# A direct column-tiled projection for the first head groups, split weight loads, and a gate logit carried as a column of v

## The chip, the cores and the metric

The kernel runs on one core of one Trainium2 chip. The time is the device time of one execution in microseconds (us). Executions of one kernel agree within one to two per cent, so a kernel is run several times and the median is given. A run more than 1.5% above the fastest of the same kernel is labelled slow, and slow runs are left out of ratios.

The engines are TensorE (PE; its weight loads are PEld), VectorE (DVE), ScalarE (ACT), GpSimd (POOL) and SyncE (SP, which here issues nearly all DMAs; its queue is SPq). Each works through a list of instructions of its own, in the order that the program gives. PEclk is the granted clock of TensorE; 1.0 is full speed. A DMA lands when its data has arrived; times to landing are counted from its issue.

## The reference, cut to what matters

The output mixes two branches of the same x (2048 rows of 640) by a gate: infini-attention (32 heads of 20, four segments of 512 rows, softmax inside a segment plus a memory of earlier ones) and a spectral filter (2-D FFT, a product, inverse FFT).

```python
x = A_x
g = sigmoid((x * gate_w).sum(-1, keepdims=True))     # one number per row
a = attention(x, wq, wk, wv, wo, beta)
b = irfft2(rfft2(x) * (w_r + 1j * w_i))
out = g * a + (1 - g) * b
# inside attention, for each of 4 segments of 512 rows and each of 32 heads:
q, k, v = x @ wq, x @ wk, x @ wv                     # 640 columns = 32 heads x 20
p = softmax(q @ k.T * scale + causal_mask)
o = sig(beta) * (phi(q) @ M) / (phi(q) @ z) + (1 - sig(beta)) * (p @ v)
M, z = M + phi(k).T @ v, z + phi(k).sum()
```

## The kernel before

The kernel is written as a list of operations with a priority each. A list scheduler turns it, before anything runs, into one fixed order per engine, by modelled costs and these priorities. So every edit can move instructions on every engine.

```python
    TSTART, TEND, F_START, F_END = 13.8, 215.6, 27.9, 227.1      # priorities: when the
    LEAD, LEAD_END, QK_LEAD, PV_LAG = 35.3, 2.6, 15.6, -2.0      # 80 exponentials are meant
    O_STEP, FIN = 1.5, (3.0, 1.0)                                # to run, and the rest round them
    def either(self, fn, n, r, w, prio, name="", after=()):      # FFT folds: DVE or GpSimd,
        return self.Sc.op({"dve": (fn, 75 + 0.6 * n, 90.0),      # whichever the cost model
                           "pool": (fn, 100 + 1.95 * n, 90.0)}, ...)    # finds earlier free
```

The start loads x transposed and then the weights, all on the SP queue; the whole of wq has to land before the first projection.

```python
    def loads(self):
        self.xt_load(0, 0.0)                     # xT of segment 0, a DMA transpose
        ...
        wload(self.wq, self.wq_d, "wq", 0.1)     # 128 x 5 x 640
        wload(self.wk, self.wk_d, "wk", 0.2)
```

The heads are 20 rows high, and this kernel gives each of them 32 partitions of its own for the attention matmuls. So q and k go out to DRAM and come back in padded rows (qp, kp), four heads to a head group, four groups to a tile. Two groups are a pair, and one pair takes five exponentials of 128 x 2048. QK is the matmul in front of an exponential (q with k), PV the one behind it (the exponentials with v). A fold is an addition or subtraction of two halves of x before the forward transform.

```python
    def project(self, s):
        for half in range(2):
            tiles = (0, 1, 2) if half == 0 else (3, 4)
            for which in ("q", "k"):
                for t in tiles:
                    self.proj_tile(s, which, t, ...)   # 5 matmuls, eviction, store to q_scr/k_scr
                for j in range(4):                      # padded reload of four groups
                    self.dma(pad.ap(0, [L, 4], [1, L], p0=32 * j, np_=32), <scr rows>, ...)
        for i in range(4):
            self.v_tile(s, i, pv, xT, xb)
        self.gate(s, t_end, xT, xb)
```

The gate is 80 matmuls of one column for each segment, arranged so that the result already has the layout that the output needs (row 16p + 4a + q).

```python
    def gate(self, s, t_end, xT, xb):
        for a in range(4):
            for c in range(5):
                for q in range(4):                     # 32 rows each, stride 16
                    matmul(ps[32 * q, a], xT.ap(c * L + 4 * a + q, [16, 32]), gw.ap(c, [1, 1]), ...)
        z[0:4] = exp(-ps)                              # ACT, then three tiny DVE operations
```

The softmax here doesn't subtract the row's maximum and nothing guards it: scores larger than these inputs give would overflow.

Of the kernel before, what the change touches and what calls it, by code (L numbers as in the profile page):

```python
# [9 lines left out]
ACT = mybir.ActivationFunctionType  # L10
ALU = mybir.AluOpType
BF = dt.bfloat16
F32 = dt.float32

P = 128
S = 2048
D = 640
H = 32
DH = 20
NSEG = 4  # L20
L = 512
# [475 lines left out]
class Kern:  # L497
# [62 lines left out]
    def either(self, fn, n, r, w, prio, name="", after=()):  # L560

        return self.Sc.op({"dve": (fn, 75 + 0.6 * n, 90.0), "pool": (fn, 100 + 1.95 * n, 90.0)}, r=r, w=w, prio=prio, name=name, after=after)

# [11 lines left out]

    TSTART, TEND, F_START, F_END = 13.8, 215.6, 27.9, 227.1
    LEAD, LEAD_END, QK_LEAD, PV_LAG = 35.3, 2.6, 15.6, -2.0
    PH, MEM0, MEMU, O_BASE = 4.0, 5.5, 1.2, 13.2
    O_STEP, FIN = 1.5, (3.0, 1.0)

# [21 lines left out]
    def alloc(self):  # L602
# [5 lines left out]
        self.kd = nc.dram_tensor("k_scr", (NSEG, 656, L), BF)  # L608
        self.od = nc.dram_tensor("o_scr", (S, D), BF)

        self.Cp = T("Cp", [P, 3 * 4096])
# [27 lines left out]
        self.wo = T("wo", [P, 5 * D])  # L639
        self.wv = T("wv", [P, 5 * D])  # L640
        self.gw = T("gw", [P, 8])
        self.xT = [T(f"xT{i}", [P, 5 * L]) for i in range(2)]
# [20 lines left out]
        self.ebx = T("ebx", [P, 4 * H], F32)  # L663
        self.gz = T("gz", [P, 64], F32)
        self.rs = [T(f"rs{i}", [P, 16], F32) for i in range(4)]
        self.dn = [T(f"dn{i}", [P, 32], F32) for i in range(4)]
# [51 lines left out]
    def loads(self):  # L718
        x = self.x

        def wload(t, d, key, prio, pitch=D):
            self.dma(lambda: t.ap(0, [pitch, 5], [1, D]), lambda: dap(d, 0, [D, P], [P * D, 5], [1, D]),
                     P * 5 * D * 2, [], [self.b(key)], prio, name="ld_" + key)
        self.xt_load(0, 0.0)
        for nm, scr in (("q", self.qd), ("k", self.kd)):
            self.dma(lambda scr=scr: dap(scr.ap(), D * L, [656 * L, NSEG], [L, 16], [1, L]),
                     lambda: dap(self.tab["fcat"].ap(), 0, [16 * L, NSEG], [L, 16], [1, L]), 64 * L * 2, [], [self.b(nm + "tail")], 0.22,
                     name="ld_tail")
        wload(self.wq, self.wq_d, "wq", 0.1)
        wload(self.wk, self.wk_d, "wk", 0.2)  # L730
        self.dma(lambda: self.fcat.ap(0, [1, 512]), lambda: dap(self.tab["fcat"].ap(), 0, [512, P], [1, 512]),
                 P * 1024, [], [self.b("fcat")], 0.9, name="ld_fcat")
        for q in range(8):
            self.dma(lambda q=q: self.xsb.ap(q * 2 * D, [D, 2], [1, D]),
                     lambda q=q: dap(x, q * 2 * D, [16 * D, P], [D, 2], [1, D]),
                     P * 2 * D * 2, [], [self.b("xsb", q)], 1.0 + 0.2 * q, name="ld_x")
        self.dma(lambda: self.beta.ap(0, [1, H]), lambda: dap(self.beta_d, 0, [0, P], [1, H]), P * 64, [],
                 [self.b("beta")], 0.25, name="ld_beta")
        wload(self.wv, self.wv_d, "wv", 0.3, D)
        self.dma(lambda: self.gw.ap(0, [1, 5]), lambda: dap(self.gw_d, 0, [1, P], [P, 5]),  # L740
                 P * 5 * 64, [], [self.b("gw")], 2.8, name="ld_gw")
        self.dma(lambda: self.big.ap(0, [1, 3216]), lambda: dap(self.tab["big"].ap(), 0, [3216, P], [1, 3216]),
                 P * 6432, [], [self.b("big")], 5.0, name="ld_big")
        self.dma(lambda: self.hm.ap(0, [1, 880]), lambda: dap(self.tab["hmask"].ap(), 0, [880, P], [1, 880]),
                 P * 1760, [], [self.b("hm")], 6.0, name="ld_hm")
        wload(self.wo, self.wo_d, "wo", 60.0)
# [50 lines left out]
    def project(self, s):  # L797
        b = self.b
        xT = self.xT[s % 2]
        xb = b("xT", s % 2)  # L800
        t_end = self.texp(s, 0)
        lead = self.LEAD if s else self.TSTART
        t0 = t_end - lead
        span = lead - self.LEAD_END if s else 2.0
        if s > 0:
            self.xt_load(s, self.texp(s - 1, 0) + 6.0 if s > 1 else 10.0)
        k = 0
        for half in range(2):
            tiles = (0, 1, 2) if half == 0 else (3, 4)
            for which in ("q", "k"):  # L810
                for t in tiles:
                    self.proj_tile(s, which, t, t0 + span * k / 10.0, xT, xb)
                    k += 1
                pad = (self.qp if which == "q" else self.kp)[(2 * s + half) % self.NPAD]
                scr = self.qd if which == "q" else self.kd
                rb = [b(which + "d", s, t) for t in (tiles if half == 0 else (2, 3, 4))] + [b(which + "tail")]
                for j in range(4):
                    def dst(j=j, pad=pad):
                        return pad.ap(0, [1, 4 * L], p0=32 * j, np_=32) if False else pad.ap(0, [L, 4], [1, L], p0=32 * j, np_=32)

                    def src(j=j, scr=scr, half=half):
                        return dap(scr.ap(), s * 656 * L + (320 * half + 20 * j) * L, [L, 32], [80 * L, 4], [1, L])
                    self.dma(dst, src, 32 * 4 * L * 2, rb, [b(which + "p", (2 * s + half) % self.NPAD, j)],
                             t0 + span * k / 10.0, name="pad_" + which)
        for i in range(4):
            pv = t0 + span * (0.3 + 0.6 * i / 4)
            if s == 0:
                pv = 2.2 + 0.2 * i
            self.v_tile(s, i, pv, xT, xb)
        self.gate(s, t_end, xT, xb)  # L830

    def gate(self, s, t_end, xT, xb):

        b, z = self.b, self.gz
        bank = Bank(1, "gen")
        prio = t_end - 2.0
        items = []
        for a in range(4):
            for c in range(5):
                for q in range(4):  # L840
                    def th(a=a, c=c, q=q):
                        return (self.ps(bank, a, [1, 1], p0=32 * q, np_=32), xT.ap(c * L + 4 * a + q, [16, 32]), self.gw.ap(c, [1, 1]),
                                c == 0, c == 4, {"tile_position": (0, 32 * q)})
                    items.append((th, 1))
        self.mms(items, [xb, b("gw"), bank], [], prio, name="gate")
        self.one("act", lambda e: e.activation(z.ap(4 * s, [1, 4]), self.ps(bank, 0, [1, 4]), ACT.Exp, scale=-1.0), 4,
                 [bank], [b("ge", s)], prio, name="gate_exp")
        self.one("dve", lambda e: e.tensor_scalar(z.ap(16 + 4 * s, [1, 4]), z.ap(4 * s, [1, 4]), 1.0, None, ALU.add), 4,
# [6 lines left out]
    def proj_tile(self, s, which, t, prio, xT, xb):  # L855
# [10 lines left out]
        for c in range(5):  # L866
            self.mms([(lambda c=c: (self.ps(bank, 0, [1, L]), w.ap(c * D + t * P, [1, P]), xT.ap(c * L, [1, L]),
                                    c == 0, c == 4, {}), L)], [b("w" + which), xb, bank], [], prio, name="proj")
        self.Sc.op(self.copy_alts(lambda: qu.ap(0, [1, L]), lambda: self.ps(bank, 0, [1, L]), L),
# [28 lines left out]

    def v_tile(self, s, i, prio, xT, xb):
        b = self.b  # L900
        va, vb = self.va[s % 2], b("va", s % 2, i)
        for (h0, nh, w) in ((0, 25, 500), (25, 7, 140)):
            self.v_part(s, i, h0, nh, w, prio, xT, xb, va, vb)

    def v_part(self, s, i, h0, nh, w, prio, xT, xb, va, vb):
        b = self.b
        bank = Bank(1, "gen")
        for c in range(5):
            self.mms([(lambda c=c: (self.ps(bank, 0, [1, w]), xT.ap(c * L + i * P, [1, P]), self.wv.ap(c * D + h0 * DH, [1, w]),
                                    c == 0, c == 4, {}), w)], [b("wv"), xb, bank], [], prio, name="vproj")  # L910
        self.one("dve", lambda e: e.tensor_tensor(  # L911
            va.ap(i * H * VW + h0 * VW, [VW, nh], [1, DH]), self.ps(bank, 0, [DH, nh], [1, DH]),
            self.ebx.ap(H + h0, [1, nh], [0, DH]), ALU.mult), nh * DH, [bank, b("omgh")], [vb], prio, name="ev_v")
    def mem_read(self, s):
        b = self.b
# [54 lines left out]
    def qk_unit(self, s, pr, u, parts):  # L970
# [5 lines left out]
        for gp, js in parts:  # L976
            g = 2 * pr + gp
            pidx, gl = (2 * s + g // 4) % self.NPAD, g % 4
            qp, kp = self.qp[pidx], self.kp[pidx]
            rb += [b("qp", pidx, j) for j in range(4)] + [b("kp", pidx, j) for j in range(4)]  # L980
            for j in js:
# [290 lines left out]
```

## Time and profile before

| | before |
|---|---|
| time, median of 3 runs | 297.97 us (297.27 to 299.27) |
| span of the profiled run | 295.0 us |
| first exponential starts | 29.4 us |
| last exponential starts | 263.0 us |

From the page of the kernel before: busy us with the share of the span, then (parts in tenths, 40 slices of 7.4 us) PE and its granted clock.

```profile
PE 255.5 (87%) x3564; PEld 152.5 (52%) x3588; DVE 213.0 (72%) x510; ACT 199.8 (68%) x183; POOL 184.1 (62%) x259
...
PE   6797367799999688899999799999899999999690
...
PEclk9799755579999699999999799999999999999997
```

PE is the busiest engine. It has a thin stretch at the start, where its clock also drops, and is nearly full from then on. The table by stretch of the same kernel (busy us of PE, PEld, DVE, ACT, POOL with counts, then PEclk, DMA share, GB/s) puts numbers on that.

```profile
0.00:30.00 30.00, 24.14 (x109) 10.45 (x110) 11.43 (x24) 9.05 (x15) 13.14 (x16) 0.94 0.81 227
...
30.00:62.00 32.00, 21.05 (x315) 14.07 (x316) 29.85 (x58) 20.24 (x18) 22.83 (x31) 0.54 0.65 161
...
120.00:270.00 150.00, 143.77 (x2139) 86.22 (x2152) 117.61 (x291) 121.63 (x104) 104.30 (x150) 0.99 0.47 109
```

From 30 to 62 us DVE is busy 29.85 of 32 us and PE runs at about half clock; from 120 to 270 us PE is busy 96%. The chain of waits of the kernel before (start us, us, what) opens with the loads.

```profile
0.80 2.75 SPq L568
...
3.62 5.20 DMA wq<-in_A_wq_dram
...
8.86 9.26 PE psum L541 x35
...
274.52 4.42 DMA oTl<-on_115
...
282.93 5.23 DMA out_dram<-ot_83
```

The issue of the transpose comes first, then wq, which lands at 8.8 us; only then do real projections start. At the end, DMAs are what is waited for: a transpose of the attention's output (oTl) and a store of the final output. The timeline of the kernel before shows the first attention matmuls, the first exponential and one gate burst.

```profile
28.94 0.40 PE L541 MATMUL psum<-qp_107,kp_109 20*128 20x512 bf16 x4 [0.48 <-DMA kp_109<-k_scr]
...
29.38 1.88 ACT L1001 ACTIVATE ex<-psum 128x2048 bf16<-128x2048 f32 x1 [6.94 <-PE psum L541]
...
51.36 1.43 PE L541 MATMUL psum<-gw,xT_96 128*32 128x1 bf16 x80
```

The first pair waits for the padded reload of k, and a gate burst takes PE 1.43 us (the three others 1.41). The trace of the kernel before lacks 24 of its 3588 matmul records (x3564 against x3588 weight loads), all of them projections of 512 columns; this matters below, where busy times are compared.

### The profile page before, as it was taken

The page shows a single profiled execution, that of the slowest core. Times are in us where ns is not written, and L with a number is a line of the kernel's source. Part 1 is how long each engine was busy: PE and PEld are TensorE (multiplying, and loading weights), DVE is VectorE, ACT ScalarE, POOL GpSimd, SP SyncE. Part 2 cuts the span into 40 slices and gives each one's busy share as a digit, 9 for nine tenths or more (in the row PEclk, how much of TensorE's full clock was granted, in tenths as well). Part 3 has the DMA queues.
Part 4 walks back from the last instruction along what each step waited for, and adds up shares of the span by engine and source line. Part 5 has one row for each costly group of instructions (what it writes and reads, how often), then busy time and mean ns, then how long its engine had stood idle before and what let it go on. Part 6 is the DMA issues. An engine that isn't in the chain of part 4 may idle for free.

```text
span 295.0 us, 8701 instructions
## 1 busy us (share of the span) xinstructions
PE 255.5 (87%) x3564; PEld 152.5 (52%) x3588; DVE 213.0 (72%) x510; ACT 199.8 (68%) x183; POOL 184.1 (62%) x259
## 2 busy tenths in 40 slices
PE   6797367799999688899999799999899999999690
PEld 2343235574557446465656456555466555555370
DVE  0049999977987589698999898884769676765251
ACT  1170556668988377998889678879778987673220
POOL 6046478876968559699878869995655462633000
PEclk9799755579999699999999799999999999999997
DMA  7869991264975958755465954234633004375622
GB/s 170 289 173 267 270 256 35 55 149 129 224 171 129 219 95 200 172 127 144 114 140 160 162 151 117 74 108 71 176 111 118 17 2 49 89 109 118 124 83 65
DMA packets 60552, 40.07 MB, mean 136 GB/s; under 512 B 33464, under 2 KB 57304, under 8 KB 60504
## 3 DMA queue, kind: packets, MB, share of 16 engines
q1 hardware_dynamic: 60512, 39.51, 55.5%
q8 instruction: 28, 0.46, 0.7%
q14 instruction: 12, 0.10, 0.1%
HBM read 22.45 MB, written 9.96 MB: 110 GB/s over the span
## 4 chain that ended last, share of the span: by engine, by line
PE 49%; DVE 21%; DMA 8%; SPq 8%; ACT 5%; POOL 3%; issue 3%; DVEq 0%
PE psum L541 49%; ACT ex L1001 5%; SPq L568 5%; DVE xsb L792 4%; SPq L570 3%; DMA kp_109<-k_scr 2%; DVE Ac L551 2%; DVE Pt_66 L1143 2%; DMA out_dram<-ot_83 2%; DMA wq<-in_A_wq_dram 2%; DVE Pt_67 L1143 2%; DMA oTl<-on_115 1%; DVE va_111 L911 1%; POOL ex L1004 1%; DVE xf_118 L787 1%
## 5 line engine op out<-in xcount | busy, mean ns | idle before, releaser
L1001 ACT ACTIVATE ex<-psum 128x2048 bf16<-128x2048 f32 x80 | 150.0, 1875 | 40.1 <-PE psum L541 39.8
L1004 POOL TENSOR_SCALAR_AFFINE_SELECT ex<-ex 128x512 bf16<-128x512 bf16 x128 | 80.8, 649 | 44.3 <-ACT ex L1001 44.2
L541 PEld LDWEIGHTS psum<-va_111,ex 128*128 128x128 bf16 x640 | 23.6, 99 | 8.9 <-POOL ex L1004 1.5
L541 PE MATMUL psum<-va_111,ex 128*128 128x21 bf16 x640 | 25.8, 175 | 1.4 <-POOL ex L1004 1.1
L541 PE MATMUL psum<-qp_107,kp_109 20*128 20x128 bf16 (+3 forms) x256 | 18.3, 344 | 10.0 <-ACT ex L1001 5.4
L541 PEld LDWEIGHTS psum<-va_112,ex 128*128 128x128 bf16 x640 | 22.7, 96 | 6.8 <-issue 2.6
L541 PE MATMUL psum<-va_112,ex 128*128 128x21 bf16 x640 | 25.1, 173 | 0.6 <-DVE Pt_66 L1143 0.5
L541 PE MATMUL psum<-big,Ac 128*128 128x321 bf16 (+2 forms) x96 | 24.2, 343 | 0.3 <-DVE Pt_67 L1143 0.2
L541 PE MATMUL psum<-wv,xT_97 128*128 128x500 bf16 (+1 forms) x80 | 22.6, 302 | 0.5 <-DVE rs_129 L1029 0.2
L541 PE MATMUL psum<-big,Cp 128*128 128x321 bf16 (+1 forms) x96 | 20.2, 302 | 0.0
L541 PE MATMUL psum<-wv,xT_96 128*128 128x140 bf16 (+1 forms) x80 | 18.3, 301 | 1.1 <-DVE va_111 L911 0.8
L541 PE MATMUL psum<-fcat,xsb 128*128 128x128 bf16 x80 | 10.7, 302 | 7.9 <-DVE xsb L792 6.1
L541 PE MATMUL psum<-xT_96,wq 128*128 128x512 bf16 x45 | 15.3, 411 | 2.5 <-DMA wq<-in_A_wq_dram 2.5
L551 DVE CAST Cp<-psum 128x512 bf16<-128x512 f32 (+1 forms) x24 | 13.4, 575 | 5.0 <-PE psum L541 4.8
L541 PE MATMUL psum<-qp_108,kp_110 20*128 20x128 bf16 (+3 forms) x256 | 15.9, 301 | 0.4 <-ACT ex L1001 0.2
L541 PE MATMUL psum<-xT_97,wk 128*128 128x512 bf16 x43 | 15.5, 379 | 0.0
L1143 DVE TENSOR_TENSOR Pt_66<-psum,Wt_62 128x321 bf16<-128x321 f32 x32 | 14.4, 481 | 1.3 <-PE psum L541 1.0
L1036 POOL TENSOR_TENSOR on_115<-on_115,mem 128x320 bf16<-128x320 bf16 x16 | 12.8, 801 | 3.8 <-DVE on_115 L1031 3.6
L1143 DVE TENSOR_TENSOR Pt_67<-psum,Wt_63 128x321 bf16<-128x321 f32 x32 | 13.8, 485 | 1.5 <-PE psum L541 1.5
L891 POOL TENSOR_TENSOR phk_104<-phk_104,et_101 128x512 bf16<-128x512 bf16 x6 | 7.0, 1159 | 12.6 <-DVE et_101 L889 12.1
L541 PE MATMUL psum<-xT_96,wk 128*128 128x512 bf16 x46 | 14.7, 382 | 0.0
L551 DVE CAST G<-psum 128x321 bf16<-128x321 f32 x25 | 11.7, 487 | 4.1 <-PE psum L541 3.9
(193 smaller groups left out, 568.1 us busy)
## 6 DMA issues: line engine op xcount, KB each, us to landing
xsb<-in_A_x_dram SPq DMA_DIRECT2D x8, 320.0 KB, 5.0
qp_107<-q_scr SPq DMA_DIRECT2D x16, 128.0 KB, 3.1
kp_109<-k_scr SPq DMA_DIRECT2D x16, 128.0 KB, 2.8
qp_108<-q_scr SPq DMA_DIRECT2D x16, 128.0 KB, 3.7
kp_110<-k_scr SPq DMA_DIRECT2D x16, 128.0 KB, 3.0
tt_59<-tab_tt SPq DMA_DIRECT2D x6, 256.0 KB, 3.2
tt_60<-tab_tt SPq DMA_DIRECT2D x5, 256.0 KB, 3.9
tt_61<-tab_tt SPq DMA_DIRECT2D x5, 256.0 KB, 3.3
```

The lines of the kernel that those rows point to most:

```text
L541: h = e.matmul(o_, l_, r_, start=st, stop=sp_, **kw)
L551: alts["dve"] = (lambda e: e.tensor_copy(dst(), src()), 75 + 1.04 * n, 85.0)
L568: return e.dma_start_transpose(d_, s_)
L570: return e.dma_start(d_, s_)
L787: self.either(lambda e, r=r, op=op: e.tensor_tensor(xf.ap(r * 642, [321, 2], [1, 320]), xs.ap(o, [D, 2], [1, 320]), xs.ap(o + 320, [D, 2], ...
L792: self.either(lambda e, dst=dst, src=src, d0=d0, n=n, op=op: e.tensor_tensor(xs.ap(o + dst, [D, 2], [1, n]), xf.ap(src + d0, [321, 2], [1, ...
L891: fadd = lambda e: e.tensor_tensor(dst(), dst(), et.ap(0, [1, L]), ALU.add)
L911: self.one("dve", lambda e: e.tensor_tensor(va.ap(i * H * VW + h0 * VW, [VW, nh], [1, DH]), self.ps(bank, 0, [DH, nh], [1, DH]), self.ebx. ...
L1001: self.one("act", lambda e: e.activation(dst(), src(), ACT.Exp, scale=SC), 4 * width, [bank], [self.exb(s, g, j) for g, j in outs], prio - ...
L1004: self.one("pool", lambda e, g=g, j=j: e.affine_select(self.ex.ap(self.exo(s, g) + JOFF[j], [1280, 4], [1, P]), self.ex.ap(self.exo(s, g) ...
L1036: self.one("pool", lambda e, g=g: e.tensor_tensor(on.ap(80 * g, [D, 4], [1, 80]), on.ap(80 * g, [D, 4], [1, 80]), self.mem.ap(80 * g, [D, ...
L1143: self.one("dve", lambda e, r=r, ri=ri, Pt=Pt, Wt=Wt, bank=bank: e.tensor_tensor(Pt.ap((2 * r + ri) * 322, [1, KD]), self.ps(bank, 0, [1, ...
```

## The change

The intent is to take three things off the front and off PE. First, head groups 0 and 1 of segment 0 are projected straight into the padded layout by four column tiles of 32, without the trip through DRAM. Second, the first 192 columns of wq and wk come as separate loads on the ACT queue. Third, the gate's 80 matmuls go: gate_w becomes column 641 of the v weights, so the logit falls out of the v projection, and a small store and reload through DRAM turns it into the layout that the output needs. The constants of the schedule were tuned anew as well, and the cost that the scheduler assumes for a fold on DVE was raised. The diff, cut to its core:

```diff
-        return self.Sc.op({"dve": (fn, 75 + 0.6 * n, 90.0), "pool": (fn, 100 + 1.95 * n, 90.0)}, ...)
+        return self.Sc.op({"dve": (fn, 75 + 0.8 * n, 90.0), "pool": (fn, 100 + 1.95 * n, 90.0)}, ...)
-    TSTART, TEND, F_START, F_END = 13.8, 215.6, 27.9, 227.1
-    LEAD, LEAD_END, QK_LEAD, PV_LAG = 35.3, 2.6, 15.6, -2.0
-    PH, MEM0, MEMU, O_BASE = 4.0, 5.5, 1.2, 13.2
-    O_STEP, FIN = 1.5, (3.0, 1.0)
+    TSTART, TEND, F_START, F_END = 9.7, 206.1, 27.9, 227.1
+    LEADS, LEAD_END, QK_LEAD, PV_LAG = (35.3, 35.3, 35.3), 2.6, 15.6, -3.5
+    PH, MEM0, MEMU, O_BASE = 4.0, 5.5, 1.1, 13.2
+    O_STEP, FIN, V0, XT1 = 1.5, (0.8, 2.6), 2.9, 11.2
 ... loads
+        wload(self.wq, self.wq_d, "wqa", 0.0, D, 0, n0, "act")           # n0 = 192
+        wload(self.wk, self.wk_d, "wka", 0.01, D, 0, n0, "act")
+        wload(self.wq, self.wq_d, "wqb", 0.1, D, n0, D - n0)
+        wload(self.wk, self.wk_d, "wkb", 0.11, D, n0, D - n0)
 ... project, segment 0 only
+            for n_, (g, which) in enumerate(((0, "q"), (0, "k"), (1, "q"), (1, "k"))):
+                self.proj_direct(which, g, -0.5 + 0.1 * n_, xT, xb)
+    def proj_direct(self, which, g, prio, xT, xb):
+        for c in range(5):
+            for hh in range(4):                      # four column tiles, one after the other
+                matmul(ps(p0=32 * hh, np_=32), w.ap(c * D + (4 * g + hh) * DH, [1, 32]),
+                       xT.ap(c * L, [1, L]), tile_position=(0, 32 * hh))
+        copy(pad.ap(g * L, [1, L]), ps)
 ... gate
-        <80 one-column matmuls and one exp per segment>
+        self.dma(lambda: dap(self.gd.ap(), s * L, [1, P], [P, 4]), lambda: self.gr.ap(4 * s, [1, 4]), 512 * 64,
+                 [b("gr", s, i) for i in range(4)], [b("gd", s)], prio, name="st_g")
+        self.dma(lambda: z.ap(4 * s, [1, 4]), lambda: dap(self.gd.ap(), s * L, [1, 4], [16, 32], [4, 4]), 512 * 64,
+                 [b("gd", s)], [b("ge", s)], prio, name="ld_g")
 ... v_part
-        for (h0, nh, w) in ((0, 25, 500), (25, 7, 140)):
+        for (h0, nh, w) in ((0, 25, 500), (25, 7, 141)):
+        if h0:
+            activation(self.gr.ap(4 * s + i, [1, 1]), self.ps(bank, 140, [1, 1]), ACT.Exp, scale=-1.0)
```

## The prediction

> **What bounds it now.** The busy table has PE 255.5 us of 295, DVE 213, ACT 200 (150 of it the 80 exponentials, 1.88 us each), and the chain of waits is 49% PE. In windows there are two regimes. From 120 to 270 us PE is 96% busy at full clock: only less PE work shortens that. Before 120 us PE is idle 23 us and runs at half clock from about 33 to 62 us (granted clock 0.5).
>
> The start is a chain of latencies. The timeline has: transpose of x issued 0.8 us, wq issued behind it at 3.6 and landed at 8.8 (first real matmul 8.86); projections; store to DRAM; padded reload; first QK at 28.9; first exponential at 29.4. ACT is busy only 0.6 us with exponentials before 30 us. From 29 to 62 us DVE is the limiter (about 95% busy from 25 to 55: FFT folds, evictions), and exponentials come one per about 3.3 us there.
>
> **Removed.** (1) The DRAM round trip for head groups 0 and 1: their five exponentials can begin at about 11-13 us rather than 29.4. (2) The gate matmuls: 4 bursts of 80, 1.4 us each by the trace: 5.7 us of PE, some 4.3 of it where PE counts. (3) Waiting for the whole of wq: half-width pieces on a second issuing queue should land near the transpose of x, at 5.5-6.5 us. The Trainium skill (DMA: Bandwidth & Descriptors, "Issuing engines are not separate DMA queues") says a second queue saves only issue time, here about 3 us.
>
> **Added.** 80 column-tiled matmuls of 512 columns. In this trace four column tiles of 320 columns go by every 0.14-0.15 us (8 in 0.46 with the drain), so I estimate 0.22-0.24 us per four at full clock: 20 x 0.23 = 4.6 us, up to 9 if cold. Four evictions (0.6 us each), 12 more tiny exponentials on ACT for the gate (0.17 us each, 2 us), 8 small 4-byte gate DMAs, 1,280 more weight packets. The full projections still run, some 4 us later unless the earlier weights pay for it. Folds move from DVE to GpSimd (1.4 against 0.41 us alone).
>
> **On the critical path.** The exponentials start 17 us earlier, but most of that does not survive: PE is already 99% busy from 10 to 25 us, and the second pair of head groups still needs the round trip (ready near 29-31 us). What survives is one pair's attention work done in formerly idle PE and ACT time. That is about 8 us of full-clock PE (QK 2-3, PV 160 x 35 ns), taken from the later saturated stretch, plus 4 us of gate, less 3-4 us of pushed-back start work. About 9 us.
>
> **Prediction: 289 us, 8 in 10 between 282 and 295.** Faster by over 2%: 0.70; within 2%: 0.25; slower: 0.05.
>
> **Signs.** First exponential at 10-14 us; first five done by 26 us; the sixth at 30-34 us. Direct-projection matmuls start 55 ns apart. No gate bursts. PE still at half clock for part of 33-60 us because folds on DVE remain the limiter. Span from the last exponential to the end as before (about 30 us). PE idle before 120 us down by 8 us or more.
>
> **What would make it wrong.** The second pair's padded rows come 5 us or more later; then the gain halves. A queue stall of SP behind the gate's store and reload. Odd-element rows of the V weights slowing the 500-column matmuls. Or, upward: PE stays warm through 33-60 us, worth several us more.

## The result, and the profile after

| | before | after |
|---|---|---|
| time, median of 4 runs | 298.62 us (297.27 to 299.64) | 334.29 us (329.44 to 334.79) |
| ratio of the fast runs | 1 | 1.112 (95%: 1.095 to 1.128) |
| first exponential starts | 29.4 us | 17.3 us |
| last exponential starts | 263.0 us | 301.5 us |

Ratios here are the mean time of one kernel's fast runs over that of the other's fast runs of the same rounds, so they are not quite the ratio of the medians quoted. The changed kernel is 11% slower. Its profile is of a run labelled slow (334.79 us; the fast runs took 334.21 and 329.44). The runs of the experiments b_gate_col and a_lat10 below show the same stalls.

The same lines of the page for the changed kernel, with the group of part 5 that is new (busy us and mean ns, then the idle time of the engine in front of it):

```profile
PE 270.1 (81%) x3348; PEld 147.8 (44%) x3348; DVE 210.3 (63%) x511; ACT 201.7 (61%) x197; POOL 186.0 (56%) x260
...
PE   5999678749898846599998089999971999999883
...
PEclk9999767969999988769999579999995599999978
...
L867 DVE TENSOR_SCALAR gz<-gz 128x4 f32<-128x4 f32 x4 | 0.7, 171 | 24.1 <-DMA gz<-g_scr 24.1
```

PE now has four holes, one in each segment. Four DVE instructions that work 0.7 us in all had DVE idle 24.1 us in front of them, for the reload of the gate. The table by stretch of the changed kernel:

```profile
0.00:30.00 30.00, 26.29 (x167) 8.54 (x168) 10.38 (x19) 12.16 (x12) 11.99 (x17) 1.00 0.71 188
...
30.00:62.00 32.00, 25.17 (x325) 15.68 (x324) 31.91 (x63) 21.40 (x28) 26.77 (x34) 0.79 0.64 166
...
120.00:270.00 150.00, 118.21 (x1437) 67.20 (x1437) 96.15 (x255) 95.44 (x84) 91.31 (x130) 0.86 0.51 105
```

The start is fuller than before, and PE's clock from 30 to 62 us is better (0.79 for 0.54). The saturated stretch is not saturated any more: PE is busy 118.21 of 150 us for 143.77. Its chain of waits names the gate and the transposes that stand near it.

```profile
0.81 6.79 DMA xT_95<-in_A_x_dram
...
7.73 15.59 PE psum L541 x117
...
58.63 12.61 DMA xT_96<-in_A_x_dram
...
125.92 10.60 SPq L568
...
136.63 3.95 DMA gz<-g_scr
...
184.83 5.53 DMA gz<-g_scr
...
242.54 10.78 DMA g_scr<-gr
...
253.34 2.93 DMA gz<-g_scr
```

Line L568 is the issue of a DMA transpose; here the queue SP stands 10.60 us on one. The gate's stores were issued at 61.5, 122.0, 174.6 and 242.5 us. The first and the fourth lie in one of these stalls, the second 3.9 us before one, and the third is followed by a reload that SP could issue only 10.2 us later, at 184.8. For SP, too, waits for the store to land before it issues the reload, and what is queued behind the reload waits with it (a line of the waits of SP: us in all, times, longest):

```profile
SPq L570 <- DMA g_scr<-gr: 15.6, 2, 7.9
```

The starts of every fifth exponential show the same four losses.

| exponential | #0 | #10 | #15 | #25 | #30 | #40 | #45 | #60 | #65 | last |
|---|---|---|---|---|---|---|---|---|---|---|
| before, us | 29.4 | 65.3 | 79.6 | 114.7 | 128.0 | 155.4 | 170.7 | 212.2 | 224.8 | 263.0 |
| after, us | 17.3 | 59.4 | 81.7 | 118.7 | 150.4 | 177.3 | 199.8 | 239.1 | 261.4 | 301.5 |

Between #10 and #15 the changed kernel loses 8 us, between #25 and #30 18, between #40 and #45 7, between #60 and #65 10. These four steps are 43 us. The head start of 12 us at #0 is 6 us at #10, before the first of them. The last line of the first timeline has no counterpart, since the gate bursts are gone; the first exponential and the direct projection look so (timeline of the changed kernel):

```profile
14.47 0.39 PE L541 MATMUL psum<-G 128*128 128x512 bf16 x1
14.79 0.40 PE L541 MATMUL psum<-xT_95,wk 128*32 128x512 bf16 x4
15.01 0.39 PE L541 MATMUL psum<-xT_95,wq 128*32 128x512 bf16 x4
15.23 0.39 PE L541 MATMUL psum<-xT_95,wk 128*32 128x512 bf16 x4
...
17.29 1.88 ACT L1025 ACTIVATE ex<-psum 128x2048 bf16<-128x2048 f32 x1 [0.48 <-PE psum L541]
```

A set of four column tiles starts 0.22 us after the one before, 54 ns a matmul. In front of them is a warm-up matmul on the full array (G), and from it to the next set are 0.32 us. Warm-ups and sets alternate up to here, until 13.7 us at a slower pace (0.54 us from start to start). "Cold" here means only such a slower start: in the kernel before, too, matmuls of 512 columns follow each other every 0.43 us at 9 to 10 us and every 0.22 us from 14 us on.

### The profile page after: what moved, and what is told of

The parts are those of the page before. It is cut to its first block, busy times and chain, and to the rows that moved or that the text cites. A ratio compares the mean times of both kernels' runs of the same rounds, so it can differ in the third digit from the quotient of the medians.

```text
span 333.1 us, 8272 instructions
## 1 busy us (share of the span) xinstructions
PE 270.1 (81%) x3348; PEld 147.8 (44%) x3348; DVE 210.3 (63%) x511; ACT 201.7 (61%) x197; POOL 186.0 (56%) x260
## 4 chain that ended last, share of the span: by engine, by line
PE 48%; DMA 17%; DVE 14%; SPq 8%; ACT 4%; issue 4%; POOL 2%; DVEq 0%
PE psum L541 48%; SPq L568 6%; ACT ex L1025 4%; DMA xT_96<-in_A_x_dram 4%; DMA gz<-g_scr 4%; DMA g_scr<-gr 3%; DMA out_dram<-ot_83 3%; DVE xsb L796 3%; SPq L570 3%; DMA xT_95<-in_A_x_dram 2%; DVE va_110 L934 1%; DVE xf_116 L791 1%; DVE phk_103 L909 1%; DVE Pt_67 L1167 1%; DVE xf_118 L791 1%
## 5 line engine op out<-in xcount | busy, mean ns | idle before, releaser
L1028 POOL TENSOR_SCALAR_AFFINE_SELECT ex<-ex 128x512 bf16<-128x512 bf16 x128 | 80.7, 647 | 64.8 <-ACT ex L1025 60.3
L541 PE MATMUL psum<-wv,xT_95 128*128 128x500 bf16 (+1 forms) x80 | 21.5, 342 | 7.6 <-DVE qu_97 L551 4.3
L541 PEld LDWEIGHTS psum<-va_111,ex 128*128 128x128 bf16 x640 | 23.7, 98 | 8.8 <-issue 3.4
L541 PE MATMUL psum<-xT_95,wq 128*128 128x512 bf16 (+1 forms) x90 | 23.3, 449 | 2.4 <-DMA xT_95<-in_A_x_dram 2.4
L541 PEld LDWEIGHTS psum<-va_110,ex 128*128 128x128 bf16 x640 | 21.7, 97 | 7.3 <-DVE va_110 L934 1.0
L541 PE MATMUL psum<-wv,xT_96 128*128 128x500 bf16 (+1 forms) x80 | 23.6, 302 | 0.0
L541 PE MATMUL psum<-xT_96,wq 128*128 128x512 bf16 x50 | 17.8, 429 | 6.7 <-DMA xT_96<-in_A_x_dram 6.6
L541 PE MATMUL psum<-big,Ac 128*128 128x161 bf16 (+2 forms) x96 | 22.2, 329 | 0.2 <-DVE Bt_64 L551 0.2
L541 PE MATMUL psum<-xT_95,wk 128*128 128x512 bf16 (+1 forms) x90 | 21.1, 406 | 0.0
L1060 POOL TENSOR_TENSOR on_114<-on_114,mem 128x320 bf16<-128x320 bf16 x16 | 12.8, 803 | 14.4 <-DVE on_114 L1055 13.7
L541 PE MATMUL psum<-xT_96,wk 128*128 128x512 bf16 x50 | 17.5, 380 | 1.8 <-ACT et_101 L898 1.3
L1172 POOL TENSOR_TENSOR Yt_69<-Pt_67 128x321 bf16<-128x321 bf16 x16 | 12.0, 764 | 9.0 <-DVE Pt_67 L1167 9.0
L1167 DVE TENSOR_TENSOR Pt_66<-psum,Wt_62 128x321 bf16<-128x321 f32 x32 | 14.9, 486 | 1.5 <-PE psum L541 1.4
L867 DVE TENSOR_SCALAR gz<-gz 128x4 f32<-128x4 f32 x4 | 0.7, 171 | 24.1 <-DMA gz<-g_scr 24.1
L551 DVE CAST qu_98<-psum 128x512 bf16<-128x512 f32 x9 | 6.2, 688 | 15.0 <-PE psum L541 13.0
## 6 DMA issues: line engine op xcount, KB each, us to landing
qp_107<-q_scr SPq DMA_DIRECT2D x16, 128.0 KB, 4.2
kp_109<-k_scr SPq DMA_DIRECT2D x16, 128.0 KB, 4.2
qp_106<-q_scr SPq DMA_DIRECT2D x12, 128.0 KB
kp_108<-k_scr SPq DMA_DIRECT2D x12, 128.0 KB, 2.5
```

Source lines behind the costliest of these rows:

```text
L541: h = e.matmul(o_, l_, r_, start=st, stop=sp_, **kw)
L551: alts["dve"] = (lambda e: e.tensor_copy(dst(), src()), 75 + 1.04 * n, 85.0)
L1028: self.one("pool", lambda e, g=g, j=j: e.affine_select(self.ex.ap(self.exo(s, g) + JOFF[j], [1280, 4], [1, P]), self.ex.ap(self.exo(s, g) ...
L1060: self.one("pool", lambda e, g=g: e.tensor_tensor(on.ap(80 * g, [D, 4], [1, 80]), on.ap(80 * g, [D, 4], [1, 80]), self.mem.ap(80 * g, [D, ...
L1167: self.one("dve", lambda e, r=r, ri=ri, Pt=Pt, Wt=Wt, bank=bank: e.tensor_tensor(Pt.ap((2 * r + ri) * 322, [1, KD]), self.ps(bank, 0, [1, ...
L1172: fn = lambda e, r=r, a0=a0, a1=a1, op=op, Pt=Pt, Yt=Yt: e.tensor_tensor(Yt.ap(r * 322, [1, KD]), Pt.ap(a0 * 322, [1, KD]), Pt.ap(a1 * 322 ...
```

## The experiments

Theory G: the gate's trip through DRAM costs the time. Rivals: the direct projection (column tiles, a later full projection), the split loads, or the new constants of the schedule. Runs named a_ are edits of the changed kernel, b_ of the kernel before; a_gate_pe_c0, c0_ and d_ are the kernel before with the direct projection and the split loads.

### One part away, one part alone

**a_gate_pe**, the changed kernel with the gate back on PE:

```diff
-        self.dma(... st_g ...); self.dma(... ld_g ...)
+        self.mms(<80 one-column matmuls>, ...); self.one("act", <exp of the four columns>)
```

> The changed kernel with its gate put back on TensorE (80 one-column matmuls a segment, no column in wv, no gate DMAs); everything else as changed. Theory G (the gate's trip through DRAM is what costs): about 290 us, between 284 and 297, and no idle stretch of all engines over 5 us around 62-71, 122-140, 180-190 and 243-256 us. Rival D (the direct projection and its reordering cost, or the new constants): stays above 320 us.

Measured: 311.78 us (308.81 to 313.08), ratio to before 1.047 (1.042 to 1.052). Neither theory had this range. The last exponential starts ahead of the kernel before (260.6 for 263.0 us); the loss comes after it, 46 us to the end for 32.

**b_gate_col**, the kernel before with only the gate as a column of v and its packed trip through DRAM:

```diff
-        self.mms(<80 one-column matmuls>, ...); self.one("act", <exp of the four columns>)
+        self.dma(dap(gd, s * L, [1, P], [P, 4]), gr.ap(4 * s, [1, 4]), ...)            # store
+        self.dma(z.ap(4 * s, [1, 4]), dap(gd, s * L, [1, 4], [16, 32], [4, 4]), ...)   # reload
```

> The kernel before with only the gate changed (logit as column 641 of v, exponential, store to DRAM, permuted reload). Theory G: 320 to 340 us, four stalls of about 10 us each after a store of the logits that takes 8 to 11 us to land. Rival D: within 2% of before, about 298 us.

Measured: 330.44 us (328.20 to 331.74), ratio 1.107 (1.102 to 1.113). Its chain of waits has all four trips on it:

```profile
58.30 12.97 DMA g_scr<-gr
...
71.29 3.69 DMA gz<-g_scr
...
108.94 9.73 DMA g_scr<-gr
...
118.69 4.79 DMA gz<-g_scr
...
181.89 9.07 DMA g_scr<-gr
...
190.98 4.08 DMA gz<-g_scr
...
242.40 9.19 DMA g_scr<-gr
...
251.61 2.99 DMA gz<-g_scr
```

The four stores are 41 us of the chain, the four reloads 16. The gate column, alone on the kernel before, makes nearly the whole loss. But without it the changed kernel is still 5% slower, so there is a second cause.

### What about the store is slow

**a_store16** keeps the changed kernel and orders the scratch by partition, so that a partition's four numbers are one piece of 16 bytes:

```diff
-        self.dma(lambda: dap(self.gd.ap(), s * L, [1, P], [P, 4]), ...
+        self.dma(lambda: dap(self.gd.ap(), s * L, [4, P], [1, 4]), ...
```

> The changed kernel, same instruction order on every engine; the scratch is laid out so that one partition's four values are neighbours: the store is 128 pieces of 16 bytes in place of 512 of 4 bytes; the reload still reads 512 pieces of 4 bytes. If the number of tiny DRAM writes is what is slow: the store lands in 2.5 to 4 us rather than 8 to 11, time 295 to 310 us. If the cost is that DMA waits for DMA at all (the order on SP): above 320 us. If the reload is the slow half: above 320 us.

**a_store64** keeps 512 pieces of 4 bytes and puts each at an address of its own, 64 bytes from the next:

```diff
-        self.gd = nc.dram_tensor("g_scr", (NSEG, L), F32)
+        self.gd = nc.dram_tensor("g_scr", (NSEG, L * 16), F32)
-        self.dma(lambda: dap(self.gd.ap(), s * L, [1, P], [P, 4]), ...
+        self.dma(lambda: dap(self.gd.ap(), s * L * 16, [16, P], [16 * P, 4]), ...
```

> The changed kernel, same instruction order on every engine; 512 pieces of 4 bytes as before, but each at its own 64-byte place in DRAM (scratch 16 times as large). If the number of tiny writes is what is slow: no change, store 8 to 11 us to land, about 334 us. If many engines writing neighbouring bytes of the same DRAM line is what is slow: store in 3 to 5 us, time 295 to 312 us.

**a_pitch16** is a_store64 with 16 bytes from one piece to the next:

```diff
-        self.gd = nc.dram_tensor("g_scr", (NSEG, L * 16), F32)
+        self.gd = nc.dram_tensor("g_scr", (NSEG, L * 4), F32)
```

> The changed kernel, same order on every engine, with 16 bytes from logit to logit in the scratch: still 512 pieces of 4 bytes a store. With 4 bytes the store lands in 9 to 11 us, with 64 in 2.1 to 2.4. If the time goes with how many pieces share 64 bytes (16, 4, 1): landing about 3.5 to 5 us, time 303 to 315 us. If it goes with the number of pieces in 512 bytes (128, 32, 8): about the same, 3.5 to 5 us. If only touching neighbours matter: as with 64 bytes, 2.1 to 2.4 us and about 302 us.

In all three the order of instructions on every engine is that of the changed kernel, so they differ from it in nothing but the addresses of the scratch.

| | pieces of the store | from piece to piece | store lands after | time, us | ratio to before |
|---|---|---|---|---|---|
| after / b_gate_col | 512 of 4 bytes | 4 bytes | 9 to 13 us | 334.29 / 330.44 | 1.112 / 1.107 |
| a_pitch16 | 512 of 4 bytes | 16 bytes | 3.2 to 4.3 us | 304.39 (2 runs) | 1.024 (1.011 to 1.037) |
| a_store64 | 512 of 4 bytes | 64 bytes | 2.1 to 2.4 us | 302.21 | 1.014 (1.009 to 1.018) |
| a_store16 | 128 of 16 bytes | 16 bytes | 1.6 to 3.7 us | 304.39 | 1.023 (1.016 to 1.031) |

The waits of a_store64 (waiter, awaited: us in all, times, longest) in place of the 24.1 us of the changed kernel:

```profile
DVE gz L867 <- DMA gz<-g_scr: 5.5, 4, 2.6
```

And its fourth store, the piece of its chain that stands in the place of the 10.78 us of the changed kernel:

```profile
220.80 2.42 DMA g_scr<-gr
```

So it is not the number of tiny writes: as many of them at another distance land in a quarter of the time, and 32 of the 36 us come back. What is slow is a store of 512 tiny writes that lie packed in 2 KB of DRAM. It is not that they touch: the 16-byte pieces of a_store16 touch as well and land in 1.6 to 3.7 us. By pieces in 64 bytes of DRAM the runs stand in order (16: 9 to 13 us; 4: 3.2 to 4.3 and 1.6 to 3.7 us; 1: 2.1 to 2.4 us), but a_store16 has fewer pieces as well. Nor is it the reload: in a_store16 it still reads 512 pieces of 4 bytes out of the same 2 KB. The Trainium skill (DMA: Bandwidth & Descriptors, "Specifications") gives 512 bytes as the least size for full rate and says that below it the DMA engine does a read-modify-write. The spread pieces are below 512 bytes as well and land in 2.1 to 2.4 us, so the rule alone does not explain the difference. If writes to the same bytes' surroundings queue up behind each other's read and write, packing would do just this; but no run shows that step, and the size within which neighbours hurt stays open (16 bytes apart, the store lands a little later than 64 apart; the intervals of the times overlap).

One large loss is left in a_store64: from exponential #25 to #30 it takes 24.8 us, where the kernel before takes 13.3. There SP stands 5.50 us on an x transpose issued 3.9 us after the gate's store, and the reload comes behind it in SP's order.

### Is it the wait, or the DMA engines

**a_lat10** leaves the packed store and tells the scheduler that both gate DMAs land 10 us later, so that nobody should have to wait for them:

```diff
+LAT = {"st_g": 10000.0, "ld_g": 10000.0}
-                    o.t1 = bw_free + 1900.0
+                    o.t1 = bw_free + 1900.0 + o.lat
```

> The changed kernel, packed scratch and slow store as it is; only the schedule is told that store and reload of the logits land 10 us later than it thought, so no engine is placed to wait for them early. If the stalls are in-order waits on an optimistic schedule: 300 to 308 us, as with the fast store. If the store holds the DMA engines for all other transfers: 315 us or more, with transfers next to it landing late.

Measured: 331.35 us (330.50 to 331.85), ratio 1.115 (1.107 to 1.122). DVE does not wait for the gate at all any more, and nothing is gained. Its chain of waits shows what happens instead.

```profile
62.96 11.15 DMA pkn<-phk
```

The statistics of the transposes of k's phase tables (pkn) show it again, first of a_lat10, then of the kernel before.

```profile
DMA to landing us min/median/max: 2.4/3.0/11.1
```

```profile
DMA to landing us min/median/max: 2.4/2.8/5.4
```

A transpose that has nothing to do with the gate takes 11.15 us to land when it is issued beside the store. The transposes into xT_96 tell the same: 4.9 us to landing in the kernel before, 14.1 us in the changed one (each trace has the landing of one of the two). SP, no longer held in front of the reload, waits 7.7 us for a load of the filter's weights that was issued just after the store. The store itself took 12.9 us. The spacing alone decides it: a_store64, with the order of the changed kernel, has its slowest transpose into pkn at 4.8 us (changed kernel: 10.2) and its slowest of x at 9.1 us (14.1). So the packed store delays other DMAs, and it does not help to let its own reader come later. That the store's pieces keep the shared DMA engines occupied fits the Trainium skill (DMA: Bandwidth & Descriptors, "Issuing engines are not separate DMA queues": all DMAs run on the same 16 engines and interleave), and the landing times agree; I did not follow single pieces.

### Rarely instead of four times

**a_once** puts the trip of a_store64 once at the end of the kernel, **a_once_c0** the same with the constants of the kernel before, and **b_gate_once** the same on the kernel before:

```diff
-        self.gate(s, t_end)            # per segment
+        self.gate()                    # once, prio 200: one store, four reloads, three DVE operations
```

> The changed kernel with the logits of all four segments stored once (64 bytes apart), reloaded near the end, and the gate made by three VectorE instructions rather than twelve: no reload stands in the SP or VectorE order in the middle. If what 64 bytes apart left (302 us) is the wait for the reload in mid stream: 290 to 296 us, and no stretch of 5 us with VectorE waiting for it. If not: about 300 us.

> The same with the constants of before. Theory C: 3 us or more faster than with the new ones. Rival P: the same within 1.5%, or slower.

> The kernel before with only the gate changed, but stored once with 64 bytes between the logits and reloaded once near the end. If the 5.7 us of gate matmuls counted where TensorE is the limit and nothing else is paid: 292 to 295 us. If the twelve extra small ScalarE instructions and the reload near the end cost as much: 297 to 300 us.

Measured: 304.68 us (ratio 1.018; its profile fell in a slow run), 301.83 us (1.011) and 305.44 us (1.029, 95%: 1.019 to 1.039). None is better than a_store64 beyond the noise (a_once_c0: 1.004 to 1.018), and between a_once and a_once_c0 the intervals overlap, so the constants decide nothing here. In a_once no wait for the gate reaches 5 us, and the time is not 290 to 296 us all the same. b_gate_once is level with the kernel before up to exponential #65 (225.0 for 224.8 us) and loses 10 us by #70 (246.9 for 237.3): the scheduler put the reload at 220 to 232 us, where DVE's order then has to wait for it. In its chain:

```profile
227.59 4.58 DMA gz<-g_scr
```

Doing the trip once does not help if its consumer stands too near behind it in DVE's fixed order (6.2 us of waiting here).

### A version that beats both

**b_gate64_lat** is the kernel before with the gate as a column of v, the 64-byte distance, and a landing time that the scheduler takes 5 us longer than its model:

```diff
+LAT = {"st_g": 5000.0, "ld_g": 5000.0}
+        self.gd = nc.dram_tensor("g_scr", (NSEG, L * 16), F32)
```

> The kernel before with the gate as a column of v, 64 bytes between logits, and the schedule told 5 us more for store and reload. If the removed gate matmuls (3 x 1.4 us in the saturated stretch) are a gain once nothing waits: 292 to 296 us. If not: 297 us or more.

Measured: 294.28 us (293.06 to 294.81), ratio 0.989 (0.983 to 0.995): about 4 us faster than the kernel before, clear of the noise, and 40 faster than the changed one. The busy line of its page, and then the statistics of its gate DMAs (store and reload together):

```profile
PE 254.5 (87%) x3268; PEld 146.8 (50%) x3268; DVE 207.5 (71%) x512; ACT 199.7 (68%) x194; POOL 184.0 (63%) x258
```

```profile
DMA to landing us min/median/max: 2.6/3.2/3.2
```

The 320 gate matmuls are gone (3268 for 3588 weight loads), and the gate DMAs whose landing the trace shows land within 3.2 us. (That trace lacks no matmul record and the one of the kernel before lacks 24, so the two busy times of PE cannot be compared.) The gain is of the size that the bursts of the kernel before allow: four of 1.4 us, three of them after 62 us, where PE counts. But the order has changed too, so the 4 us are not shown to be the bursts.

### The second cause: constants

**a_gate_pe_c0** is a_gate_pe with the constants of the kernel before, so the kernel before with the direct projection and the split loads. **b_const** is the kernel before with the constants of the changed one.

```diff
# b_const (a_gate_pe_c0 is the reverse, on a_gate_pe)
-    TSTART, TEND, F_START, F_END = 13.8, 215.6, 27.9, 227.1
+    TSTART, TEND, F_START, F_END = 9.7, 206.1, 27.9, 227.1
-    O_STEP, FIN = 1.5, (3.0, 1.0)
+    O_STEP, FIN = 1.5, (0.8, 2.6)          # and PV_LAG, MEMU, V0, XT1, the fold cost
```

> The changed kernel with the gate on TensorE and all of its scheduling constants put back to those of before (start and end of attention, lag of PV, final tiles, fold cost): so before plus the direct projection and the split weight loads, nothing else. Theory C (the new constants cost what the gate on TensorE run lost, 46 us from the last exponential to the end against 32): about 290 to 297 us with a tail near 32 us. Rival P (the direct projection costs more than its head start brings): 303 us or more with the tail near 32 us and the last exponential later than 263 us.

> The kernel before with only the scheduling constants of the changed kernel. Theory C: 305 to 312 us, with the loss after the last exponential. Rival P: within 2% of before.

Measured: a_gate_pe_c0 300.69 us, ratio 1.007 (1.000 to 1.014); b_const 304.95 us, ratio 1.021 (1.014 to 1.028). In b_const the last exponential starts 4.7 us earlier than in the kernel before (258.3 for 263.0 us) and the kernel still ends 8.5 us later (span 303.5 us). Its chain of waits ends so:

```profile
275.99 4.83 DMA out_dram<-ot
...
281.95 5.13 DMA out_dram<-ot
...
292.39 5.13 DMA out_dram<-ot
```

Three output stores of 5 us stand one behind the other, because the output tiles have only three buffers and each waits for its store; in the kernel before it is one (282.93 above). In all, DVE waits 17.5 us for output stores in b_const and 0.9 in the kernel before. The constants bring the attention forward and bunch the output at the end. The loss of a_gate_pe is of the same kind: 17.1 us of such waits, and a tail from the last exponential to the end of 46 us, where b_const has 45. The changed kernel itself does not show it: its tail is 31.6 us (before: 32), and that of a_store64 31.3. In both the last exponential comes later (301.5 and 269.8 us), which may leave the output time to go out; that was not tested.

### Where the head start goes

With the constants of before, the direct projection starts exponentials 15 us earlier and loses 0.7%, just at the edge of the noise (1.000 to 1.014). Four theories were tried on that.

**b_split**, only the split weight loads on the kernel before:

```diff
-        wload(self.wq, self.wq_d, "wq", 0.1)
+        wload(self.wq, self.wq_d, "wqa", 0.0, D, 0, 192, "act")
+        wload(self.wq, self.wq_d, "wqb", 0.1, D, 192, D - 192)      # and wk
```

> The kernel before with the split weight loads alone (192 columns of wq and wk on the second queue, the rest behind the transpose of x). First real matmul at 8 to 9 us as before, since the plain projections need both pieces. Expected 297 to 299 us, no change; 294 or less would mean that the loads alone are worth something, 301 or more that they are what cost the direct version its gain.

Measured: 297.95 us, ratio 0.999 (0.991 to 1.008). Split loads alone neither cost nor bring.

**b_tinyfold** and **d_tinyfold** shrink the FFT folds to 2 x 4 elements, on the kernel before and on a_gate_pe_c0. Both give a wrong result. Theory V: DVE, full with folds from 30 to 62 us, eats the head start.

```diff
-                xf.ap(r * 642, [321, 2], [1, 320]), xs.ap(o, [D, 2], [1, 320]), ...
+                xf.ap(r * 642, [321, 2], [1, 4]), xs.ap(o, [D, 2], [1, 4]), ...
```

> Wrong result on purpose. The kernel before with every FFT fold shortened to 2 x 4 elements, same instructions in the same order: takes about 15 us of VectorE (and GpSimd) time out of the stage from 24 to 58 us. Baseline for the next run. Theory V (VectorE's folds limit that stage): 280 to 292 us, exponential number 11 well before 60 us. Otherwise 295 us or more.

> Wrong result on purpose. The direct projection with gate on TensorE and constants of before (300.7 us, no gain), with the same shortened folds. Theory V (the head start of the first head groups is lost because the stage to 60 us lasts as long as VectorE's folds and evictions): now the head start survives and this is at least 5 us faster than before with shortened folds. Rival P (it is lost to the pushed-back projections and the added TensorE work): no faster than that kernel, within 2 us, or slower.

Measured: 290.84 us (ratio 0.978) and 295.52 us (0.995). DVE's folds do cost the kernel before some 6 us, but with hardly any folds the direct projection stands still further behind, 4.7 us. Of theory V the first half holds (folds limit that stage), the second, that they eat the head start, falls.

**d_lean** takes away what the direct projection pushes back: fewer warm-up matmuls, and no plain projection of the first tile of q (whose heads are mostly done already).

```diff
-    NWARM = 16
+    NWARM = 9
+                    if s == 0 and which == "q" and t == 0:
+                        k += 1
+                        continue
```

> The direct projection with gate on TensorE and constants of before, less the waste before the first projections end: 9 warm-up matmuls in place of 16 (7 of them stood between the direct ones) and no plain projection of the q columns 0 to 127 of segment 0, which nothing reads any more. Theory P (the head start is lost because projections and V are pushed back, V's first matmul from 21 to 26.5 us): V about 3.5 us earlier and 295 to 298 us rather than 300.7. If the push-back is not it: 300 to 302 us.

Measured: 304.39 us, ratio 1.020 (1.011 to 1.029), slower still, though the first exponential comes at 13.5 us. That speaks against theory P, but the test was weak: the first v matmul came at 24.5 us, 2.0 us earlier and not 3.5. In all versions up to here the first exponential of segment 1 (#20) starts 39 to 40 us after the last matmul of the forward transform's first stage: 60.2 and 100.3 us in the kernel before, 59.2 and 98.5 in a_gate_pe_c0, 63.1 and 101.9 in d_lean. Segment 1's projections stand behind that transform in PE's order, since their x arrives late. This gave theory W: the lead is lost against that wall.

**b_xt** and **c0_xt** load x of segment 1 earlier, on the kernel before and on a_gate_pe_c0:

```diff
-            self.xt_load(s, self.texp(s - 1, 0) + 6.0 if s > 1 else 10.0)
+            self.xt_load(s, self.texp(s - 1, 0) + 6.0 if s > 1 else 2.9)
```

> The kernel before with one edit: the transpose of x for segment 1 gets a priority that places it right after the eighth load of x rows (ahead of the transposes of the phase tables), so that segment 1's projections may be scheduled among the forward transform of segment 0. It is the base for c0_xt. Theory W (segment 1's start hangs on this load and on the projections that stand behind the forward transform on TensorE, so a lead of segment 0 is lost at the gap between exponentials 19 and 20): that exponential comes at least 5 us earlier than the 100.3 us of the kernel before; the time moves by 0 to -4 us. Rival (TensorE's total work sets when segment 1 can start, whatever the order): exponential 20 within 3 us of 100.3, time within 1%.

> The direct projection and split weight loads alone on the kernel before's constants and gate (as in a_gate_pe_c0, 300.7 us and 0.7% slower than before), with the same early transpose of x for segment 1 as in b_xt. Theory W: with the gap removed the lead of segment 0 passes on: exponential 20 comes at least 3 us ahead of that of b_xt and the time is at least 3 us below that of b_xt. Rival (the lead is paid for with TensorE work that is due later, the direct matmuls and the interrupted order, whatever happens at the gap): exponential 20 within 2 us of b_xt or later, and the time 0 to 5 us above b_xt, as a_gate_pe_c0 stood 2 us above the kernel before.

Measured: b_xt 295.96 us (fast runs 293.6 to 296.8), ratio 0.991 (0.977 to 1.005), so unclear; c0_xt 299.25 us, ratio 1.000 (0.985 to 1.015). c0_xt's profile is of a slow run. The start of exponential #20 in b_xt, then in c0_xt (timelines):

```profile
92.97 1.88 ACT L1001 ACTIVATE ex<-psum 128x2048 bf16<-128x2048 f32 x1 [1.72 <-PE psum L541]
```

```profile
96.14 1.88 ACT L1031 ACTIVATE ex<-psum 128x2048 bf16<-128x2048 f32 x1 [3.19 <-PE psum L541]
```

The wall was real: in b_xt exponential #20 comes 7 us earlier than in the kernel before, 28 us after the transform. (The last exponential is then hardly earlier, 262.3 for 263.0 us, so most of those 7 us were lost again later.) But the second half of theory W falls: with the wall gone the direct projection still does not keep its lead. It is 3 us behind at #20, and 1.8 us behind in the mean of the fast runs (297.0 for 295.2 us; the intervals overlap, so the times alone do not decide it). This is what the rival foretold. That the lead is paid for with PE work is argued from the busy times that follow, not shown: d_lean, which takes PE work away, is slower. The stretch from 0 to 62 us of a table by stretch, first b_xt, then c0_xt:

```profile
0.00:62.00 62.00, 47.98 (x475) 25.13 (x475) 41.95 (x88) 31.26 (x33) 36.57 (x47) 0.81 0.78 196
```

```profile
0.00:62.00 62.00, 51.70 (x534) 24.48 (x535) 37.58 (x81) 33.11 (x36) 34.88 (x44) 0.92 0.73 185
```

PE is busy 3.7 us longer there, at a better clock, and yet the work of segment 0 and the transform is done later (last matmul of that first stage 69.2 us for 64.8). In the whole run PE is busy 267.9 us in c0_xt and 259.1 in b_xt, 8.8 us more. As c0_xt's profile is of a slow run, pairs of fast ones count more: 263.9 for 257.2 us in d_tinyfold against b_tinyfold (no records missing), and 264.5 in a_gate_pe_c0 for 255.5 in the kernel before (24 projections missing in both). So the direct projection adds some 7 to 9 us of busy PE, and what the head start brings does not exceed what is lost. The order shows what they push back: the first v matmul comes at 26.5 us in a_gate_pe_c0 and 21.2 in the kernel before, and the padded reload of k is issued at 28.8 us for 21.6. So the first exponentials start, and then wait for all that stands behind: in a_gate_pe_c0 the fourth starts at 37.3 us, in the kernel before at 41.5.

## Why the prediction was wrong, point by point

The prediction was 289 us with 0.05 for slower; it is 334.

- **"8 small 4-byte gate DMAs" without a cost: this is the step that failed.** They were listed under what is added and entered no sum. They are worth 32 us on the kernel before (b_gate_col), and 32 of the changed kernel's 36 us go away with another distance between the same writes (a_store64), for the store then lands in 2.1 to 2.4 us instead of 9 to 13 and holds up DVE (5.5 us for 24.1) and the transposes beside it far less. What the prediction took from the trace was the number of instructions; it did not ask how long a store of 512 packed 4-byte pieces takes, and no line of the profile before could have told. The skill's rule that a strided last dimension lowers to one descriptor per element (DMA: Bandwidth & Descriptors, "Rules for kernel authors") said that each of these is 512 pieces, and the runs agree: from the kernel before to b_gate_col, which differs in the gate alone, the packets rise by 4174 (60552 to 64726), and four stores and four reloads of 512 pieces are 4096. The prediction's warning of "a queue stall of SP behind the gate's store and reload" named the place (SP stands 10.60 us on one issue), but it had no number and no share of the chances.
- **"What survives is one pair's attention work … about 8 us": failed.** The first exponential came at 17.3 us, not 10 to 14; five were not done by 26 us (the fifth started at 40.2), and the sixth started at 42.6, not 30 to 34. The lead at #10 was 6 us in the changed kernel, and in a_gate_pe_c0, without the trip of the gate, it is 2.7 us at #10 and gone at #30 (128.0 us in both). The direct projection costs PE 7 to 9 us of busy time (the pairs above), and with the split loads it makes the kernel 0.7% slower (1.000 to 1.014). Which of its costs eats the lead stays open. The prediction's own "what would make it wrong", second padded rows 5 us or more late, came true (7 us late in a_gate_pe_c0), but what followed was no halved gain: it was none.
- **The added direct matmuls, "4.6 us, up to 9 if cold": at the upper end, 7 to 9 us in the pairs above.** Warm ones did start 54 ns apart as estimated. In the changed kernel the early ones, between warm-up matmuls, went at 0.54 us from start to start. And a set that follows a full-array matmul starts 0.32 us behind it instead of 0.22; the Trainium skill (TensorEngine Tiling (Array Packing), "Key Properties") says that changing the tiling mode drains TensorE, and this trace agrees with about 0.1 us at each change.
- **The schedule's constants had no term.** They cost 2.1% on the kernel before (b_const). Their parts do not add up: a_gate_pe carries constants and direct projection at 4.7%, more than the 2.1% and 0.7% of each alone, and a_store64 carries both and the gate column at 1.4%. A fixed order for all engines is not a sum of parts.
- **"The gate matmuls … some 4.3 of it where PE counts": right.** Once the trip is cheap and its readers stand far enough behind, b_gate64_lat gains about 4 us.
- **"A second queue saves only issue time, here about 3 us": no gain at all by itself** (b_split, 0.999). In the changed kernel xT landed at 7.6 us, not at the 5.5 to 6.5 foreseen: the pieces on the second queue may have slowed it, since by the section of the Trainium skill that the prediction names (DMA: Bandwidth & Descriptors) all DMAs share the same engines, but no run separates this.
- **Small signs.** No gate bursts, a tail of 31.6 us (said: about 30) and no harm from 141 columns of v (median of the v matmuls 319 to 349 ns; 348 in a_gate_pe_c0, with 140 columns) are as foretold. "PE idle before 120 us down by 8 us" is wrong: it is 23 us in both. PE's clock from 30 to 62 us was better than foretold (0.79), and it did not help.

Open stay: the exact size within which neighbouring tiny writes disturb each other, and by what mechanism; which part of the pushed-back work loses the lead, since d_lean, which has less of it (first v matmul 24.5 us for 26.5), is slower; and a loss of about 5 us that a_gate_pe_c0 takes between exponentials #55 and #65 (from 197.4 for 196.8 us to 230.3 for 224.8), far from any edit. Differences of 1% between versions here are in part those of another fixed order, which no run separates.

## What to carry to other kernels

A DMA that looks tiny by its bytes has to be costed by its pieces and by where they land: before a trip through DRAM is put into a loop, measure its landing and that of the DMAs beside it, and try giving small pieces addresses of their own, further apart (64 bytes here). Work that starts earlier by extra work on the engine that is nearly full may be paid for there; look whether the engine was idle in that stretch, not on the average. And if a schedule is one fixed order, run each part of a change alone, for a re-tuned constant can cost as much as the part that it was tuned for.

## What the Trainium skill lacked or had wrong

- DMA: Bandwidth & Descriptors gives a least size for full rate, but not that the landing of tiny writes depends on the distance between them: 512 pieces of 4 bytes land in 9 to 13 us packed, in 3.2 to 4.3 us at 16 bytes from piece to piece, in 2.1 to 2.4 us at 64.
- The same page says that DMAs interleave on shared engines; it has no number for what a DMA beside such a store loses: beside the packed store a transpose took 11.15 us to land (median 2.8 in the kernel before), and SP stood 10.60 us on the issue of one.
- The same page's rule for a strided last dimension is to rearrange it. Where that is not to be had, spreading the pieces helps as much (a_store64 302.21 us, with 16-byte pieces 304.39), which the page does not say.
- TensorEngine Tiling (Array Packing) says that a change of mode drains the array, without a figure: 0.32 us from a full-array matmul to a set of column tiles, 0.22 from set to set, so about 0.1 us a change at 512 columns.
